# The start of a two-stage kernel: decoding w_in and the first values' maxima placed behind the keys' and queries' maxima, and idle products in place of products on fresh exponentials

## The chip, the cores and the metric

The kernel runs on one core of a Trainium2 chip. The metric is the device time of one execution in microseconds (us). Before the change the median of 3 runs is 954.96 us (954.61 to 955.23).

## What is computed

The reference is attention with random features, followed by a two-layer network with Mish as its activation. Batch 8, 8 heads, 576 positions, head size 64, 128 features; the network takes 4608 rows of 512 and has 2048 hidden units.

```python
def phi(x):
    h = einsum('bhsd,md->bhsm', x, omega) - sum(x * x) / 2
    return exp(h - max(h)) / sqrt(m)
q_p, k_p = phi(q * scale), phi(k * scale)
kv  = einsum('bhsm,bhsd->bhmd', k_p, v);   z = sum(k_p, axis=2)
num = einsum('bhsm,bhmd->bhsd', q_p, kv);  den = einsum('bhsm,bhm->bhs', q_p, z) + 1e-6
x = (num / den), as 4608 x 512
h = x @ w_in
out = (h * tanh(log1p(exp(h)))) @ w_out
```

The two weights arrive as float64, 8 MB each, and are read as integer words.

## The kernel before

**Stages.** Rows are taken in tiles of 128 (q0, q1, ...) and in chunks of 256 (two tiles) for the network. Keys come in pairs of heads: k0 to k3 of the first batch, then k1_0 to k1_3 of the second, and so on. Of a pair of heads, TensorE makes the products with omega (`pk`, line 377), VectorE takes the maximum of each group (`mxk`, line 387), ScalarE makes the exponentials from it (`ek`, line 392), and TensorE multiplies these with the values (`pkv`, line 451); ScalarE copies the sum to SBUF (`kvf`). A tile of queries goes the same way (`pq`, `mxq`, `eq`), and then through `q_first`: transposes of the exponentials (`pt`, line 626), ScalarE's copy (`qp`), the products with kvf (`pn`, line 637), and VectorE's division (`rd`, `x`, lines 641 to 647). x of q0 and q1 is transposed (`px`, `xT`), and with it begins the network's first chunk in f32: `ph`, line 731, takes the decoded blocks of w_in. Its result is copied to the tile `g`. The later chunks use three f16 products each with a weight split in two, for which the scale `s_w` must be known.

**The weights.** A block of w_in (8 of 1024 words per partition, `w_task`) is decoded in four steps: ScalarE's Prelu on the high word (line 184), VectorE's shift of the low word (line 186), VectorE's shift and or (line 190), and VectorE's maximum over the block (`wmax`, line 194). The eight maxima give `am_w` and `s_w`. The tiles are called w_103 to w_110, in the rows of the order with their number, in the trace `w`; the raw words lie in `wo` (the first four) or `raw`.

**The values.** `v_task` takes the maxima of the four value tiles (`vmx`, line 285), then their maximum (`vam`), and from it the scale `s_v` through GpSimd.

**What sets the order.** Every engine works through its instructions strictly in the order in which they are queued. Tasks are Python generators that are stepped in slots: the number they yield says in how many slots they go on. `FIRST` gives the slots of the attention's tasks, `WIS` those of w_in's blocks. Inside these, a scheduler orders the instructions by its own estimates, except that an instruction issued inside `behind(nth)` is put behind the anchors of task nth on the same schedule. An anchor is a pair: the task's last exponential and its last maximum. 3 is the last pair of heads of the first batch, 5 is q1, 31 is the division of q1's x, 101 the second copy of xT. `AV` holds the anchor for `vmx`, `AN` the one of each block for lines 186 and 190, `AM` for line 194, `AP` for line 184; None leaves an instruction free.

**Spare products.** `spin(n, left, right)`, line 96, issues n products that nobody reads. `spin(1, ident, e[:, 0:2])`, line 404, follows the exponentials of the tasks 2 to 5 (k2, k3, q0, q1) and so waits for them. Eight others with the constant tile `idle` stand behind the second pair's products (line 383).

**Buffers that matter.** The exponentials' tile `e` has two buffers; the pool `ps_a` has four PSUM slots, which pk, pq, pkv, pt and pn share.

Of the kernel before, what the change touches and what calls it, by code (L numbers as in the profile page):

```python
# [30 lines left out]
def tile_kernel(  # L31
# [10 lines left out]
    nc = tc.nc  # L42
    P = 128
# [49 lines left out]
    idle = const.tile([P, 512], F16, name="idle")  # L93
    dve.memset(idle, 1.0)

    def spin(n, left, right):
        pi = ps_o.tile([P, 512], F32, tag="o", name=f"spin{nc.next_id()}")
        for _ in range(n):
            nc.tensor.matmul(out=pi[:, 0:right.shape[1]], lhsT=left, rhs=right, start=True, stop=True)
# [3 lines left out]
    ident = const.tile([P, P], F32, name="ident")  # L103
# [156 lines left out]
    for i in range(2):  # L260
        t = const.tile([P, 2, 10, D1], F16, name=f"vb{i}")
# [13 lines left out]
    def v_task(b):  # L275
        vt = []
        for hp in range(HP):
            vt.append(loaded.pop(f"v{b}_{hp}", None) or fetch_v(b, hp))
        if b == 0:
            vstate[0] = (vt, None, None)  # L280
        yield 3 if b else 6
        mx = sb.tile([P, HP], F32, tag="vmx", name=f"vmx{b}", bufs=2)
        for hp in range(HP):
            with behind(AV if b == 0 else None, 1):
                dve.tensor_reduce(
                    out=mx[:, hp:hp + 1], in_=vt[hp][:, :, 0:D], axis=AX.XY, op=ALU.max,
                    apply_absolute_value=True,
                )
            yield 0 if hp % 2 == 0 or b == 0 else 1
        am = sb.tile([P, 1], F32, tag="vam", name=f"vam{b}")  # L290
        with tc.high_priority(PRIO):
            dve.tensor_reduce(out=am, in_=mx, axis=AX.X, op=ALU.max)
            p, s = pow2(am, f"v{b}", TOP)
        vstate[b] = (vt, p, s)
# [42 lines left out]
    def features(load, tiles, name, nth, whole):  # L337

        f = loaded.pop(name, None) or (
            fetch_pair if whole else fetch_tails if name[0] == "k" else fetch
        )(load, name)
        yield gap("load", name)
        if not whole:
            terms = yield from in_parts(f, name, nth)
        n = sum(len(g) for g in tiles)
        by_act = whole
        e = sb.tile([P, n, M], F32, tag="ae", name=f"e{name}", bufs=2)
        mx = sb.tile([P, n], F32, tag="mx", name=f"mx{name}")  # L350
        pps, lo = [], 0
        for g in tiles:
            own, tag = (ps_h, "h") if nth < HP and len(pps) == 2 else (ps_a, "a")
            pp = own.tile([P, 4, M], F32, tag=tag, name=f"p{name}_{lo}")
            pps.append((pp, lo, lo + len(g)))
            lo += len(g)
            if whole:
                continue
            for i, parts in enumerate(g):
                for rows, o in parts:  # L360
                    for j, (left, right) in enumerate(terms):
                        nc.tensor.matmul(  # L362
                            out=pp[rows, i, :], lhsT=left[:, o:o + rows.stop - rows.start],
                            rhs=right, start=j == 0, stop=j == len(terms) - 1,
                        )
        if whole:

            w = f.shape[1]
            order = [(g, i) for i in range(4) for g in (0, -1)] + [(1, 0)] * (len(tiles) - 2)
            mm = None  # L370
            for g, i in order:
                for rows, o in tiles[g][i]:
                    a = slice(o // w * D, (o // w + 1) * D)
                    with ExitStack() as st:
                        if mm is not None:
                            st.enter_context(tc.issue_after(mm.ins))
                        mm = nc.tensor.matmul(
                            out=pps[g][0][rows, i, :], lhsT=f[a, o % w:o % w + rows.stop - rows.start],
                            rhs=om_f[a], start=True, stop=True,
                        )  # L380
            if nth == 1:
                with tc.issue_after(mm.ins):
                    spin(8, idle[:, 0:P], idle)
        yield 1
        for pp, lo, hi in pps:
            m = hi - lo
            sub = dve.tensor_reduce(  # L387
                out=mx[:, lo:hi], in_=pp[:, :m, :], axis=AX.X, op=ALU.max, negate=by_act
            )
            if by_act:  # L390
                for i in range(m):
                    last = act.activation(
                        e[:, lo + i, :], pp[:, i, :], AF.Exp, bias=mx[:, lo + i:lo + i + 1]
                    )
            else:
                sub = dve.tensor_tensor(  # L396
                    out=e[:, lo:hi, :], in0=pp[:, :m, :],
                    in1=mx[:, lo:hi].unsqueeze(2).broadcast_to([P, m, M]), op=ALU.subtract,
                )
        yield gap("exp", name)  # L400
        if not by_act:
            last = act.activation(e, e, AF.Exp, bias=lnt)  # L402
        elif 1 < nth < 6:
            spin(1, ident, e[:, 0:2, :].rearrange("p n m -> p (n m)"))
        anchors[nth] = (last.ins, sub.ins)
        return e

# [211 lines left out]
    def q_first(nth, t, e, off):  # L619

        qp = sb.tile([P, H, P], F32, tag="ap", name=f"qp{t}", bufs=2)
        for g in range(2):
            hs = slice(4 * g, 4 * g + 4)
            pt = ps_a.tile([P, 4, P], F32, tag="a", name=f"pt{t}_{g}")
            for i in range(4):
                nc.tensor.transpose(out=pt[:, i, :], in_=e[:, 4 * g + i, :], identity=ident)
            cast(act, qp[:, hs, :], pt)
        yield 1
        x = sb.tile([P, H, D], F32, tag="x", name=f"x{t}", bufs=2)
        rd = sb.tile([P, H, 1], F32, tag="rd", name=f"rd{t}")  # L630
        for g in range(2):
            hs = slice(4 * g, 4 * g + 4)
            pn = ps_a.tile([P, 4, D1], F32, tag="a", name=f"pn{t}_{g}", padded_shape=[P, 4, P])
            for i in range(4):
                for b, lo, hi in spans(t * P, P):
                    must(HP, "kvf", b)
                    nc.tensor.matmul(
                        out=pn[lo:hi, i, :], lhsT=qp[:, 4 * g + i, lo:hi], rhs=kvf[b][:, 4 * g + i, :],
                        start=True, stop=True,
                    )  # L640
            dve.tensor_scalar(
                out=rd[:, hs], in0=pn[:, :, D:D1], scalar1=EPS, scalar2=1.0 if t * P < CH else TOP / TX,
                op0=ALU.add, op1=ALU.mult,
            )
            dve.reciprocal(out=rd[:, hs], in_=rd[:, hs])
            if t * P < CH:
                xt = dve.tensor_tensor(
                    out=x[:, hs, :], in0=pn[:, :, 0:D], in1=rd[:, hs].broadcast_to([P, 4, D]),
                    op=ALU.mult,
                )  # L650
                continue
            for b, lo, hi in spans(t * P, P):
                xt = dve.scalar_tensor_tensor(
                    out=x[lo:hi, hs, :], in0=pn[lo:hi, :, 0:D], scalar=vstate[b][2][lo:hi],
                    in1=rd[lo:hi, hs].broadcast_to([hi - lo, 4, D]), op0=ALU.mult, op1=ALU.mult,
                )
        anchors[30 + t] = (xt.ins,)
        if t * P >= CH:
            yield from x_parts(nth, t, x)
            return  # L660
        yield 1
        px = ps_a.tile([P, KT, P], F32, tag="a", name=f"px{t}")
        for i in range(KT):
            nc.tensor.transpose(out=px[:, i, :], in_=x[:, 2 * i:2 * i + 2, :], identity=ident)
        last = act.activation(xT0()[:, :, off:off + P], px, AF.Copy)
        anchors[100 + t] = (last.ins,)
        did("x", 0)
        if t == 1:
            for hs in (slice(0, 4), slice(4, 8)):
                spin(1, ident, x[:, hs, :].rearrange("p h d -> p (h d)"))  # L670
# [265 lines left out]
    w_dma = nc.sync  # L936

    FIRST = (0, 1, 2, 3, 4, 4, 9, 9, 19, 21, 24, 27, 32, 36, 43, 58, 59, 68)
    WIS = (3, 4, 5, 6, 7, 8, 9, 10)
    WOS = (28, 27, 26, 25, 24, 23, 22, 21)  # L940
    WI0, FF0, V0, V1 = 0, 17, 0, 16
    W_LOAD, W_GAP, PRIO = 1, 1, 400

    AO = (None,) * 8
    AV = 3
    AN = (None,) * 5 + (31,) * 3
    AM = (None,) * 3 + (31,) * 5
    AP = (None,) * 7 + (101,)

    W_LO = ('dddddddd', 'dddddddd')  # L950
    W_HI = ('aaaaaaaa', 'aaaaaaaa')
# [90 lines left out]
    for what in PREL.split():  # L1042
        i = int(what[1:] or 0)
# [100 lines left out]
```

## Time and profile before

| | |
|---|---|
| median of 3 runs | 954.96 us |
| profiled execution | 955.38 us, its span 953.6 us, mean granted clock 0.989 |
| PE (TensorE) busy | 929.1 us, 97% of the span |
| DVE (VectorE) busy | 625.7 us, 66% |
| ACT (ScalarE) busy | 636.8 us, 67% |
| POOL (GpSimd) busy | 220.6 us, 23% |
| DMA | 100.25 MB, mean 105 GB/s |
| first 20 us | PE 18.53, DVE 7.67, ACT 10.65 us busy |

The chain that ended last, followed back from the last instruction, names `po`, the second layer's products of line 900, with 12% of the span, and PE with 22% in all. Over the whole span TensorE is nearly always busy; the stretch that the change touches is the first 60 us of 954. All times in the text are counted from the start of the span. Instructions of one kind that follow each other stand in one row of the timeline, with their count behind an x; an f32 product is recorded as two instructions. "PEclk" is the clock that TensorE was granted, as a share of full speed.

### The profile page before, as it was taken

The numbers are of one execution on the slowest core, as the hardware profiler recorded it, in microseconds if no ns is written. First come the engines' busy times: TensorE is split into PE (matmuls) and PEld (weight loads), VectorE is DVE, ScalarE is ACT, GpSimd is POOL, SyncE is SP. The second block draws the span as 40 slices with busy tenths as digits, with TensorE's granted clock in tenths as the row PEclk, the third lists the DMA queues.
The fourth block names the chain that finished last, engine by engine and source line by source line (L and its number), as shares of the span: only waits on it lengthen the run. The fifth ranks groups of instructions, "written<-read, shape, count | busy, mean of one in ns | idle before, by whom it ended". The sixth has DMA issues, their size and how long they took to land. (4 is left out here: it accounts for less than half of the span.)

```text
span 953.6 us, 20400 instructions
## 1 busy us (share of the span) xinstructions
PE 929.1 (97%) x8558; PEld 667.8 (70%) x8558; DVE 625.7 (66%) x1080; ACT 636.8 (67%) x821; POOL 220.6 (23%) x141
## 2 busy tenths in 40 slices
PE   9799989999999999999999999999999999999998
PEld 6688765676777777777777777777756777776663
DVE  4799887686665766656564664789889656643330
ACT  5668975678878777787677775778686866432231
POOL 0000042344333222332232323313232231100000
PEclk9799999999999999999999999999999999999999
DMA  9766333432532355224332353324542155644410
GB/s 307 255 221 213 96 82 82 92 82 61 131 79 63 84 104 103 60 62 93 72 68 73 73 114 70 83 78 104 123 113 67 34 115 106 169 129 130 128 63 25
DMA packets 148443, 100.25 MB, mean 105 GB/s; under 512 B 112320, under 2 KB 124736, under 8 KB 148352
## 3 DMA queue, kind: packets, MB, share of 16 engines
q1 hardware_dynamic: 148032, 98.36, 40.7%
q8 instruction: 67, 1.10, 0.5%
q10 hardware_dynamic: 320, 0.59, 0.2%
q14 instruction: 24, 0.20, 0.1%
HBM read 58.95 MB, written 13.63 MB: 76 GB/s over the span
## 5 line engine op out<-in xcount | busy, mean ns | idle before, releaser
L900 PE MATMUL po<-wo,g 128*128 128x512 f16 x1632 | 375.2, 380 | 0.0
L731 PE MATMUL ph<-xT,w 128*128 128x256 f16 (+1 forms) x2816 | 343.9, 278 | 2.7 <-ACT h L876 2.7
L731 PEld LDWEIGHTS <-w 128*128 128x128 f16 x2688 | 261.8, 98 | 51.4 <-issue 4.1
L900 PEld LDWEIGHTS <-g 128*128 128x128 f16 x1632 | 155.2, 98 | 163.9 <-issue 2.2
L83 DVE SCALAR_TENSOR_TENSOR g<-h,us,g 128x1024 f16<-128x1024 f32 (+3 forms) x92 | 117.5, 1287 | 35.8 <-ACT g L72 35.2
L876 ACT ACTIVATE h<-ph,us 128x512 f32<-128x512 f32 (+3 forms) x152 | 83.2, 572 | 75.0 <-PE ph L731 74.1
L81 POOL TENSOR_TENSOR sq<-fq,sq 64x1024 f16<-64x1024 f32 x31 | 69.3, 2238 | 159.1 <-issue 86.8
L81 POOL TENSOR_TENSOR sk<-fk,sk 64x1152 f16<-64x1152 f32 x24 | 60.5, 2519 | 124.1 <-ACT sk L72 99.6
L81 POOL TENSOR_TENSOR xs<-x,xs 128x512 f16<-128x512 f32 (+1 forms) x35 | 43.4, 1241 | 145.1 <-issue 66.7
L72 ACT ACTIVATE g<-h,us 128x1024 f16<-128x1024 f32 (+3 forms) x80 | 72.6, 932 | 1.2
L876 ACT ACT_TABLE_LOAD x56 | 71.8, 1283 | 1.0
L402 ACT ACT_TABLE_LOAD x53 | 68.0, 1283 | 4.2 <-DVE ek L396 3.3
L387 DVE TENSOR_REDUCE mxq<-pq 128x4 f32<-128x512 f32 x72 | 46.8, 681 | 26.6 <-PE pq L362 25.7
L81 DVE TENSOR_TENSOR qn<-eq,qn 128x1024 f16<-128x1024 f32 x31 | 39.5, 1275 | 37.2 <-ACT qn L72 37.2
L834 PEld LDWEIGHTS <-w 128*128 128x128 f16 x1008 | 58.4, 98 | 5.9
L387 DVE TENSOR_REDUCE mxk<-pk 128x4 f32<-128x512 f32 (+1 forms) x96 | 49.5, 548 | 17.7 <-PE pk L362 8.3
L876 ACT ACTIVATE h<-h,us 128x1024 f32<-128x1024 f32 (+2 forms) x16 | 14.7, 933 | 62.0 <-DVE h L843 62.0
L72 ACT ACTIVATE o<-po,us 128x512 f32<-128x512 f32 (+1 forms) x38 | 25.8, 679 | 40.5 <-PE po L900 40.5
L81 DVE TENSOR_TENSOR kp<-ek,kp 128x1152 f16<-128x1152 f32 x24 | 36.8, 1534 | 24.0 <-ACT kp L72 24.0
L402 ACT ACTIVATE eq<-eq,lnt 128x1024 f32<-128x1024 f32 x31 | 35.6, 1148 | 22.1 <-DVE eq L396 21.9
L843 DVE TENSOR_TENSOR h<-p_s,h 128x512 f32<-128x512 f32 x30 | 20.2, 689 | 43.2 <-PE p_s L834 43.2
L81 POOL TENSOR_TENSOR vb<-vf,vb 128x640 f16<-128x640 f32 x24 | 38.7, 1614 | 41.9 <-DVE vb L74 28.1
(143 smaller groups left out, 1140.2 us busy)
## 6 DMA issues: line engine op xcount, KB each, us to landing
w<-ds SPq DMA_DIRECT2D x48, 256.0 KB, 3.4
vf<-in_vL_dram SPq DMA_DIRECT2D x32, 325.0 KB, 3.3
out_dram<-o SPq DMA_DIRECT2D x36, 256.0 KB, 2.3
fq<-in_qT_dram SPq DMA_DIRECT2D x31, 256.0 KB, 3.5
fk<-in_kT_dram SPq DMA_DIRECT2D x24, 256.0 KB, 3.6
raw<-in_w_out_dram SPq DMA_DIRECT2D x5, 1024.0 KB, 7.9
wo<-in_w_in_dram SPq DMA_DIRECT2D x4, 1024.0 KB, 10.7
raw<-in_w_in_dram SPq DMA_DIRECT2D x4, 1024.0 KB, 15.3
```

What stands on the lines that cost most here:

```text
L72: act.activation(out, in_, AF.Copy, scale=scale)
L81: eng.tensor_tensor(out=out, in0=in_, in1=hi, op=ALU.subtract)
L83: eng.scalar_tensor_tensor(out=out, in0=in_, scalar=scale, in1=hi, op0=ALU.mult, op1=ALU.subtract)
L387: sub = dve.tensor_reduce(out=mx[:, lo:hi], in_=pp[:, :m, :], axis=AX.X, op=ALU.max, negate=by_act)
L402: last = act.activation(e, e, AF.Exp, bias=lnt)
L731: nc.tensor.matmul(out=ph[:, i, :], lhsT=wi(a, k, f) if c else wi0(k, f), rhs=xT[c][:, y, k, :] if c else xT0()[:, k, :], start=n == 0, st ...
L834: nc.tensor.matmul(out=ph[:, i, :], lhsT=left(gr, op_l, i, a, k), rhs=x_region(c, r)[:, y, k0 + k, :], start=n == 0, stop=n == len(mm) - 1,)
L843: dve.tensor_tensor(out=out, in0=bank, in1=in0, op=ALU.add)
L876: act.activation(h[:, :, lo:hi], ph[:, :, lo:hi], AF.Mish, scale=us[:, 0:1])
L900: nc.tensor.matmul(out=po[i], lhsT=gT[c, gr][:, a, f % FG, i * P:(i + 1) * P], rhs=wo(y, f), start=f == 0 and (a, y) == parts[0], stop=f = ...
```

## The change

The change edits three places and one group of tables:

- Line 281: the values' task of the first batch goes on one slot later (7 for 6).
- Lines 403 and 404: the product on the fresh exponentials of k2, k3, q0 and q1 is gone.
- In `q_first`, for q0 and q1: 6 and 3 products on the constant tile `idle`, behind the tile's last transpose.
- The tables: w_in's blocks start one or two slots later; `vmx` stands behind q1's maxima; lines 186 and 190 of block 0 stand behind k3's maxima, of block 1 behind q1's, and of the six others behind q1's x; line 194 of block 0 behind k3's maxima, and of all others behind q1's x; the Prelu of blocks 2 to 6 behind q1's last exponential and maximum.

```diff
-        yield 3 if b else 6
+        yield 3 if b else 7
...
             last = act.activation(e, e, AF.Exp, bias=lnt)
-        elif 1 < nth < 6:
-            spin(1, ident, e[:, 0:2, :].rearrange("p n m -> p (n m)"))
         anchors[nth] = (last.ins, sub.ins)
...
-                nc.tensor.transpose(out=pt[:, i, :], in_=e[:, 4 * g + i, :], identity=ident)
+                tr = nc.tensor.transpose(out=pt[:, i, :], in_=e[:, 4 * g + i, :], identity=ident)
             cast(act, qp[:, hs, :], pt)
+        if t < 2:
+            with tc.issue_after(tr.ins):
+                spin(6 - 3 * t, idle[:, 0:P], idle)
...
-    AV = 3
-    AN = (None,) * 5 + (31,) * 3
-    AM = (None,) * 3 + (31,) * 5
-    AP = (None,) * 7 + (101,)
+    AV = 5
+    AN = (3, 5) + (31,) * 6
+    AM = (3,) + (31,) * 7
+    AP = (None,) * 2 + (5,) * 5 + (101,)
```

VectorE's row from the last maximum of k3 to the first of q0, before (mxk_3 is k3's, mxq_330 q0's; w_104 is block 1 of w_in, w_105 block 2):

```order
L387 TENSOR_REDUCE mxk_3_283<-pk_3_5_286 128x4
L285 TENSOR_REDUCE vmx_353<-vf_0_135 128x1
L285 TENSOR_REDUCE vmx_353<-vf_1_137 128x1
L285 TENSOR_REDUCE vmx_353<-vf_2_139 128x1
L285 TENSOR_REDUCE vmx_353<-vf_3_141 128x1
L190 SCALAR_TENSOR_TENSOR w_104<-wo,w_104 128x1024
L292 TENSOR_REDUCE vam_358<-vmx_353 128x1
L186 TENSOR_SCALAR w_105<-wo 128x1024
L134 TENSOR_SCALAR p_v_362<-allm_v_360 128x1
L194 TENSOR_REDUCE wmax_121<-w_104 128x1
L123 TENSOR_SCALAR p_v_362<-p_v_362 128x1
L387 TENSOR_REDUCE mxq_330<-pq_0_331 128x4
```

The same place now, on VectorE, from k3's last maximum on (mxq_320 is q0, mxq_332 q1):

```order
L387 TENSOR_REDUCE mxk_3_278<-pk_3_5_281 128x4
L190 SCALAR_TENSOR_TENSOR w_103<-wo,w_103 128x1024
L194 TENSOR_REDUCE wmax_121<-w_103 128x1
L387 TENSOR_REDUCE mxq_320<-pq_0_321 128x4
L387 TENSOR_REDUCE mxq_320<-pq_4_322 128x4
L387 TENSOR_REDUCE mxq_332<-pq_0_333 128x4
L387 TENSOR_REDUCE mxq_332<-pq_4_334 128x4
L285 TENSOR_REDUCE vmx_416<-vf_0_135 128x1
```

The four maxima of the queries moved ahead of the values' maxima and of blocks 1 and 2. Block 0's lines 190 and 194, which now stand ahead of the queries, stood a few rows further up, between k3's maxima.

TensorE's row behind the products pq of q0 and q1, before (`spin` is a spare product, and what stands behind its arrow is what it reads):

```order
L377 MATMUL pq_4_344<-om_f,fq_146 128x128
L99 MATMUL spin_395<-eq_329,ident 128x256
L451 MATMUL pkv_3_373<-vf_3_141,ek_3_282 128x65 x10
L626 MATMUL pt_0_398<-ident,eq_329 128x128 x4
L99 MATMUL spin_421<-eq_341,ident 128x256
L626 MATMUL pt_1_404<-ident,eq_329 128x128 x4
L626 MATMUL pt_0_424<-ident,eq_341 128x128 x4
L626 MATMUL pt_1_430<-ident,eq_341 128x128 x4
L637 MATMUL pn_0_443<-kvf_162,qp_397 128x65 x4
```

The same place on TensorE now, up to the idle products behind q0's transposes:

```order
L377 MATMUL pq_4_334<-om_f,fq_146 128x128
L449 MATMUL pkv_3_346<-vf_3_141,ek_3_277 128x65 x10
L624 MATMUL pt_0_368<-ident,eq_319 128x128 x4
L624 MATMUL pt_1_374<-ident,eq_319 128x128 x4
L99 LDWEIGHTS idle
L99 MATMUL spin_381<-idle 128x512
L99 LDWEIGHTS idle
L99 MATMUL spin_381<-idle 128x512
```

The product on q0's exponentials ahead of pkv is gone, so is the one on q1's between q0's two groups of transposes, and six idle products follow q0's second group; three more follow q1's.

On VectorE, behind the last part of q1's x, stood before (x_459 is q1's):

```order
L647 TENSOR_TENSOR x_459<-pn_1_469,rd_460 128x256
L194 TENSOR_REDUCE wmax_121<-w_106 128x1
L194 TENSOR_REDUCE wmax_121<-w_107 128x1
L186 TENSOR_SCALAR w_108<-raw_155 128x1024
L186 TENSOR_SCALAR w_109<-raw_157 128x1024
```

And there stands now, on VectorE, behind q1's x:

```order
L648 TENSOR_TENSOR x_452<-pn_1_462,rd_453 128x256
L194 TENSOR_REDUCE wmax_121<-w_104 128x1
L186 TENSOR_SCALAR w_105<-wo 128x1024
L186 TENSOR_SCALAR w_106<-wo 128x1024
L190 SCALAR_TENSOR_TENSOR w_105<-wo,w_105 128x1024
L190 SCALAR_TENSOR_TENSOR w_106<-wo,w_106 128x1024
L194 TENSOR_REDUCE wmax_121<-w_105 128x1
L194 TENSOR_REDUCE wmax_121<-w_106 128x1
L186 TENSOR_SCALAR w_107<-raw_153 128x1024
```

Behind x come now the decoding of blocks 2 and 3 and the shift of block 4, which stood ahead of it. On TensorE, in the first chunk's products ph, 13 of blocks 0 and 1 stand ahead of the products pq of q2, where one stood.

More of the change, by code (lines that the diff above doesn't have):

```diff
@@ L938, in tile_kernel @@
     FIRST = (0, 1, 2, 3, 4, 4, 9, 9, 19, 21, 24, 27, 32, 36, 43, 58, 59, 68)
-    WIS = (3, 4, 5, 6, 7, 8, 9, 10)
+    WIS = (4, 6, 7, 8, 9, 10, 11, 12)
     WOS = (28, 27, 26, 25, 24, 23, 22, 21)
```

## The prediction, made before the run

> **What bounds the kernel now.** I read the busy time by stretch first, then TensorE's waits, then the timeline of 14 to 50 us, and last its later parts. The rows of busy time are cut at the steps of the granted clock, which come every 3.41 us; behind each stretch stand its length, the busy time of PE, PEld, DVE, ACT and POOL with instructions, the granted clock and the DMA share.
>
> ```profile
> 23.81:27.22 3.41, 0.07 (x2) 0.00 (x0) 3.41 (x7) 2.69 (x4) 0.00 (x0) 1.00 1.05 388
> 27.22:30.63 3.41, 0.00 (x0) 0.00 (x0) 3.14 (x8) 0.52 (x3) 0.62 (x1) 0.50 1.05 389
> 30.63:34.05 3.42, 3.26 (x14) 3.08 (x14) 3.42 (x7) 2.69 (x8) 0.00 (x0) 0.50 1.05 385
> 34.05:37.46 3.41, 3.41 (x15) 3.08 (x16) 3.31 (x4) 1.02 (x3) 0.00 (x0) 0.50 1.07 267
> 37.46:40.87 3.41, 3.41 (x16) 2.69 (x14) 0.40 (x1) 2.83 (x9) 0.00 (x0) 0.50 1.03 327
> ...
> 45.53:94.44 48.91, 48.44 (x316) 40.24 (x315) 47.05 (x74) 37.10 (x69) 0.70 (x2) 1.00 0.65 212
> ...
> 94.44:163.80 69.36, 64.39 (x453) 43.38 (x451) 56.68 (x104) 53.03 (x76) 15.68 (x10) 0.98 0.33 85
> ...
> 133.04:136.45 3.41, 0.92 (x9) 0.82 (x9) 2.69 (x5) 3.38 (x5) 1.99 (x2) 1.00 0.38 94
> 136.45:139.86 3.41, 3.41 (x19) 2.42 (x17) 1.08 (x3) 2.31 (x3) 1.34 (x1) 0.50 0.62 175
> ```
>
> TensorE stands still from 23.9 to 30.8 us and then runs at half clock until 40.87. From 45.53 to 94.44 both TensorE (48.44 of 48.91) and VectorE (47.05) are full, so a gain made ahead of that stretch has to pass two full engines. The waits of TensorE name who holds it (total, times, longest):
>
> ```profile
> PE spin L99 <- ACT eq L392: 6.9, 1, 6.9
> ...
> PE ph L731 <- ACT h L876: 2.7, 1, 2.7
> PE pn L533 <- DMA qp<-qn: 1.8, 1, 1.8
> ```
>
> ScalarE's exponentials of q0 are late, and ScalarE itself waits. The timeline says for what (start, length, engine, line, operation; in brackets idle time and releaser):
>
> ```profile
> 18.75 0.69 DVE L387 TENSOR_REDUCE mxk<-pk 128x4 f32<-128x512 f32 x1 [1.36 <-PE pk L377]
> 18.96 2.44 PE L451 MATMUL pkv<-vf,ek 128*128 128x65 f32 x20
> ...
> 21.24 0.65 PE L99 MATMUL spin<-ek,ident 128*128 128x256 f32 x2
> ...
> 21.82 2.06 PE L377 MATMUL pq<-om_f,fq 64*128 64x128 f32 x32
> ...
> 23.02 2.99 DVE L285 TENSOR_REDUCE vmx<-vf 128x1 f32<-128x640 f32 x4
> ...
> 25.92 1.22 DVE L190 SCALAR_TENSOR_TENSOR w<-wo,w 128x1024 int32<-128x1024 int32 x1
> ...
> 27.12 0.68 DVE L186 TENSOR_SCALAR w<-wo 128x1024 int32<-128x1024 int32 x1
> ...
> 28.15 1.21 DVE L194 TENSOR_REDUCE wmax<-w 128x1 f32<-128x1024 f32 x1
> ...
> 29.33 0.68 DVE L387 TENSOR_REDUCE mxq<-pq 128x4 f32<-128x512 f32 x1
> ...
> 30.11 2.17 ACT L392 ACTIVATE eq<-pq,mxq 128x128 f32<-128x128 f32 x8 [3.09 <-DVE s_v L125]
> ...
> 30.79 1.22 PE L99 MATMUL spin<-eq,ident 128*128 128x256 f32 x2 [6.92 <-ACT eq L392]
> ...
> 31.80 4.37 PE L451 MATMUL pkv<-vf,ek 128*128 128x65 f32 x20
> ...
> 40.69 3.77 PE L637 MATMUL pn<-kvf,qp 128*128 128x65 f32 x32
> ...
> 45.11 0.42 DVE L647 TENSOR_TENSOR x<-pn,rd 128x256 f32<-128x256 f32 x1
> ...
> 46.98 0.70 PE L731 MATMUL ph<-xT,w 128*128 128x256 f32 x2
> ```
>
> The products pq of both queries are done at 23.88, but VectorE works through the values' maxima and the decoding of w_in first and takes their maxima only at 29.33. Behind that, pkv takes 4.37 us at half clock where it took 2.44 at full, and the first hidden products ph start at 46.98.
>
> **The change, part by part.** The sum goes against the profiled execution: 955.38 us, of which 953.6 is the span and 1.8 lies around it. The median of the runs is 954.96, so 0.42 comes off at the end. 0.2% is 1.9 us, about what a measurement here can tell from no change.
>
> *Maxima first.* The first maximum of k3 moves up by the dropped product on exponentials ahead of pk: 18.75 - 0.65 = 18.1. The three maxima follow each other (0.6, 0.2, 0.6) to 19.5; one L190 and one wmax stay ahead of the queries. Neighbouring rows overlap by a little under 0.1 us (wmax from 28.15 would end at 29.36, yet q0's maximum starts at 29.33), so a step of 1.22 counts 1.13 and one of 0.68 counts 0.6: to 21.8; the queries' maxima follow. From maximum to exponential is 30.11 - 29.33 = 0.78, so eq starts at 22.65 instead of 30.11: 7.5 us earlier.
>
> *No product on exponentials ahead of pkv.* pkv of k3 still waits for the first four exponentials, since it takes the PSUM slot of pq; four of 2.17 / 8 = 0.27 end at 23.8. TensorE's pause shrinks from 6.92 to about 1 us, pkv runs at 2.44 and ends at 26.3 instead of 36.2.
>
> *Idle products.* Six behind q0's transposes and three behind q1's cost, by these rows from elsewhere in the profile (eight of the same shape; four transposes at full clock):
>
> ```profile
> 9.17 1.90 PE L99 MATMUL spin<-idle 128*128 128x512 f16 x8
> ...
> 57.74 0.60 PE L626 MATMUL pt<-ident,eq 128*128 128x128 f32 x4
> ...
> 71.65 7.17 PE L731 MATMUL ph<-xT,w 128*128 128x256 f32 x32
> ```
>
> 9 x 0.24 = 2.1 us, against 4 x 0.60 of transposes. Most of it lies in the wait for q1's exponentials: its buffer comes free with pkv's end, so they run from 26.4 to 28.6, and the transposes of q1 end near 30.9. Uncovered is the last group of three, 0.7. So pn starts at 31.55 where it was 40.69, 9.1 earlier, x is done 4.84 behind it (45.53 - 40.69) at 36.4 and, with one decoding Prelu of ScalarE now ahead of the last copy of xT, ph starts at 38.2, 8.8 earlier.
>
> *What VectorE owes then.* Behind x now stand five steps of 1.13 and three of 0.6 more than before, 7.45 us. VectorE is thus at the old point of its work at 36.4 + 7.45 = 43.85 instead of 45.53: a lead of 1.7 where TensorE leads by 8.8. The wait for w blocks is short (TensorE multiplies the first blocks while VectorE decodes the next, some 0.5 us lost). Eleven ph instructions of 7.17 / 16 = 0.45 now precede pn of q2, 4.9 us of work, and pn of q2 starts near 57.8 instead of 61.17: a lead of 8.3. It breaks at the first head of the second batch:
>
> ```profile
> 61.17 3.68 PE L637 MATMUL pn<-kvf,qp 128*128 128x65 f32 x32
> ...
> 74.22 1.48 DVE L387 TENSOR_REDUCE mxk<-pk 128x4 f32<-128x512 f32 x3
> ...
> 77.50 2.43 ACT L392 ACTIVATE ek<-pk,mxk 128x128 f32<-128x128 f32 x9
> ...
> 78.76 1.52 PE L377 MATMUL pk<-om_f,fk 64*128 64x128 f32 x18
> ...
> 80.21 2.45 PE L451 MATMUL pkv<-vf,ek 128*128 128x65 f32 x20
> ```
>
> Before, the exponentials end at 79.93 and pkv follows at 80.21, without a pause. After, VectorE reaches these maxima near 71.8 and ScalarE ends near 77.3, only 2.6 earlier, while TensorE has nothing left from 70.1: I get a new pause of 4.7 us, to 74.8. This is the change's own bill. The lead is 2.9 at the next pkv and 1.9 where the f16 products begin (94.44 before, 92.6 after).
>
> *The later waits.* From 94.44 to the start of q7's products (the last row below) the orders of all engines come together again, so what stands there stays to the end.
>
> ```profile
> 135.53 4.44 PE L731 MATMUL ph<-xT,w 128*128 128x256 f16 x24 [2.66 <-ACT h L876]
> ...
> 145.18 0.92 PE L533 MATMUL pn<-kv,qp 128*128 128x65 f16 x24 [1.77 <-DMA qp<-qn]
> ...
> 163.80 1.05 PE L362 MATMUL pq<-om,sq 128*128 128x128 f16 x16
> ```
>
> TensorE has 64.39 us of work there in 69.36, and 1.7 of the work is the second half-clock window (136.45 to 139.86, behind a window with 0.92 busy). At full clock it is 62.7. In the new order the third head's exponentials follow the second's with no Mish between, two of ScalarE's table changes fewer, and eq of q4 comes near 110 instead of 115; I keep 1.2 for the transposing DMA ahead of pn and 0.5 for the rest. 92.6 + 62.7 + 1.7 = 157.0 against 163.8: 6.8 earlier.
>
> *The clock.* The new pause of 4.7 us can cover a clock step. The rows show that a step with 0.07 or 0.92 us busy is followed by half clock, and this pause leaves such a step for most positions of the steps. The price has two ends: one step of 3.41, half of it lost, 1.7 (136.45), or four steps as from 27.22, three of them with work, 5.1. I take 1.7: as at 136.45, long runs of ph stand right behind.
>
> The Trainium skill, page "TensorE: Matmul & The Clock Gate", section "Part 1: The HAM clock gate", says that the clock halves after one idle window of some 3.4 us and returns after one busy one, with windows that run free of the kernel. By that rule the pause would cost an estimated 1.7 us. The first half of the rule agrees with 27.22 and 136.45; the second differs from the rows of 30.63 and 34.05, busy 3.26 and 3.41 us and followed by half clock all the same.
>
> Sum: -6.8 + 1.7 = -5.1, so 950.3 profiled, 949.9 as a median; I say 950.0. What lies outside these terms I cost at nothing: the decoded blocks' scale comes near 61.8 instead of 61.1, hidden by the f32 chunk, which uses no scaled block.
>
> **The rivals.**
>
> *VectorE alone decides (0.20).* With 47.05 of 48.91 busy it passes on only its own 1.7 us, and the later waits stay, since they hang on ScalarE, which waits for VectorE's splits. 955.38 - 1.7 - 0.42 = 953.3. For it: the full row. Against: VectorE idles 12.7 of the 69.36 us from 94.44.
>
> *The whole lead survives (0.12).* If the head's exponentials come as early as TensorE does, 8.8 stays: 954.96 - 8.8 = 946.2. Against it: the chain through ScalarE's Mish and two table loads ahead of 77.50.
>
> *The half clock feeds itself (0.10).* The pause near 70 to 75 halves the clock, and the f32 products of the second batch, of the kind that stayed at half clock from 30.63 on, don't lift it; every head's pause prolongs it. Each step costs 1.7, so from the fifth it is slower than before in the sum (6.8 - 8.5); six, to about 95 us, give 954.96 - 6.8 + 10.2 = 958.4. The page's rule, one busy window and it is over, speaks against so many; the rows of 30.63 to 40.87 speak for it.
>
> *It doesn't do what it says (0.08).* pkv still waits for q0's exponentials through its PSUM slot; if these come no earlier, because w0's decoding or its load holds VectorE ahead of them, only the dropped products count: within a microsecond of 955.
>
> **How the numbers follow.** The forecast has 0.50, with its own range of 948.0 to 952.5 (clock price 0 to 3.4, the pause off by a microsecond). Faster by over 0.2% means under 953.05: the forecast, the second rival and over half of the first, 0.74. Within: the rest of the first, most of the fourth, 0.15. Slower: the third and a little of the fourth, 0.11. The range, 946.5 to 956.0, leaves out the edge of the second rival and most of the third.
>
> **What would show it.** Right: eq near 22.7, pkv at 2.44 us, clock 1.00 from 14 to 60, ph at 38, a pause of TensorE of some 5 us at 70 to 75 released by ek, and q7's products near 158 to 159. Wrong: TensorE paused by w blocks between 40 and 60 (VectorE decides), no pause at 70 (the lead survives), clock 0.50 for over 14 us (slower), or eq still near 30.

## The result, and the profile after

The changed kernel takes 961.88 us (median of 6 runs, 959.89 to 963.64), the kernel before, on the same chip, 955.10 (6 runs, 954.19 to 955.66). The ratio is 1.0072 with a 95% interval of 1.0058 to 1.0086: slower by 0.7%, where 950.0 was forecast. The profiled execution took 961.23 us, its span 959.4 against 953.6 before. One run of e3 below, 1066.19 us at a granted clock of 0.849 where every other run here has 0.981 or more, is left out of its ratio.

The start went as forecast. TensorE's rows in the timeline of the kernel after:

```profile
23.92 2.45 PE L449 MATMUL pkv<-vf,ek 128*128 128x65 f32 x20 [1.12 <-ACT eq L392]
...
30.88 3.68 PE L638 MATMUL pn<-kvf,qp 128*128 128x65 f32 x32
...
37.19 1.13 PE L732 MATMUL ph<-xT,w 128*128 128x256 f32 x4 [0.79 <-ACT xT L666]
...
72.30 1.52 PE L377 MATMUL pk<-om_f,fk 64*128 64x128 f32 x18 [2.19 <-ACT ek L392]
74.99 4.53 PE L449 MATMUL pkv<-vf,ek 128*128 128x65 f32 x20 [1.17 <-ACT ek L392]
...
86.09 2.45 PE L449 MATMUL pkv<-vf,ek 128*128 128x65 f32 x20
```

The first 6.9 us of waiting are down to 1.12, pkv runs at full clock, and ph starts at 37.19 instead of 46.98: 9.8 us earlier. At 72 to 75 the new pause stands, 2.19 + 1.17 us, released by ek. At the second batch's next pkv (86.09, before 87.83) 1.7 us of the lead are left. Up to here nothing is slower than before.

The loss comes later. TensorE's rows of the kernel after, around the tiles q5, q6 and q7 (before: pn of q5 at 145.18, pn of q6 at 163.04, pq of q7 at 163.80):

```profile
136.63 1.50 PE L531 MATMUL pn<-kv,qp 128*128 128x65 f16 x24 [2.88 <-DMA qp<-qn]
137.94 1.85 PE L362 MATMUL pq<-om,sq 128*128 128x128 f16 x16
139.63 13.95 PE L918 MATMUL po<-wo,g 128*128 128x512 f32 x32
157.39 1.50 PE L531 MATMUL pn<-kv,qp 128*128 128x65 f16 x24 [3.81 <-DMA qp<-qn]
158.70 5.21 PE L918 MATMUL po<-wo,g 128*128 128x512 f32 x6
163.74 3.60 PE L918 MATMUL po<-w,g 128*128 128x512 f32 x8
167.18 1.06 PE L362 MATMUL pq<-om,sq 128*128 128x128 f16 x16
```

pn of q5 now starts 8.6 us earlier than before, so the early lead is there. But pn of q6 then waits 3.81 us for its transposing DMA, with 14 records of po (6 and 8, 8.8 us of work) queued behind it that need nothing from it. They run after the wait, and q7's products start at 167.18, 3.4 us later than before. The waits of TensorE between 100 and 200 us say the same in a row:

```profile
PE pn L531 <- DMA qp<-qn: 6.7, 2, 3.8
```

Before, the two were 1.8 and 0.55. In the changed kernel one step of half clock follows the first of them, two the second. Busy time by stretch of the kernel after, at the steps of the clock (columns as in the prediction):

```profile
74.78:78.19 3.41, 3.20 (x15) 3.20 (x16) 3.41 (x5) 3.26 (x4) 0.00 (x0) 0.50 0.61 203
78.19:81.61 3.42, 3.05 (x11) 2.48 (x11) 3.42 (x6) 2.05 (x7) 0.00 (x0) 0.50 0.30 65
81.61:85.02 3.41, 3.41 (x13) 2.38 (x13) 3.41 (x4) 2.56 (x7) 0.00 (x0) 0.50 0.09 33
...
136.20:139.61 3.41, 2.98 (x40) 2.99 (x41) 2.43 (x11) 1.55 (x2) 0.00 (x0) 0.50 0.02 5
...
156.68:160.09 3.41, 2.70 (x26) 2.13 (x27) 1.89 (x6) 0.00 (x0) 0.00 (x0) 0.50 0.63 196
160.09:163.51 3.42, 3.42 (x5) 1.35 (x4) 1.37 (x4) 1.01 (x1) 0.00 (x0) 0.50 0.00 0
```

The first three rows lie behind the new pause at 72 to 75 us. What stands differently is TensorE's row behind the pq of q6. Equal rows are drawn together here, with their count ahead. Before:

```
12 L533 MATMUL pn_1_1376<-kv_674,qp_1318 128x65        (q5)
 8 L362 MATMUL pq_0_1409<-om,sq_1320 128x128           (q6)
 8 L362 MATMUL pq_4_1418<-om,sq_1320 128x128
...
 1 L917 MATMUL po_0_1390<-wo,g_0_634 128x512 x2
 1 L917 MATMUL po_1_1391<-wo,g_0_634 128x512 x2
 1 L917 MATMUL po_0_1390<-w_110,g_0_634 128x512 x2
 1 L917 MATMUL po_1_1391<-w_110,g_0_634 128x512 x2
12 L533 MATMUL pn_0_1460<-kv_674,qp_1450 128x65        (q6)
```

After:

```
 1 L918 MATMUL po_0_1391<-wo,g_0_635 128x512
12 L531 MATMUL pn_0_1461<-kv_675,qp_1451 128x65        (q6)
12 L531 MATMUL pn_1_1474<-kv_675,qp_1451 128x65
 1 L918 MATMUL po_0_1391<-wo,g_0_635 128x512
 1 L918 MATMUL po_1_1392<-wo,g_0_635 128x512 x2
 1 L918 MATMUL po_0_1391<-w_110,g_0_635 128x512 x2
 1 L918 MATMUL po_1_1392<-w_110,g_0_635 128x512 x2
 8 L362 MATMUL pq_0_1534<-om,sq_1520 128x128           (q7)
```

The change doesn't touch this place, 120 us behind its last edit. The scheduler orders by its own estimates, and with the changed start it places pn of q6 ahead of seven po instructions (14 records) behind which it stood before. Which estimate tips it isn't shown.

### The profile page after: what moved, and what is told of

The parts are those of the page before. It is cut to its first block, busy times and chain, and to the rows that moved or that the text cites. A ratio compares the mean times of both kernels' runs of the same rounds, so it can differ in the third digit from the quotient of the medians.

```text
span 959.4 us, 20405 instructions
## 1 busy us (share of the span) xinstructions
PE 931.9 (97%) x8559; PEld 669.5 (70%) x8559; DVE 629.3 (66%) x1080; ACT 633.8 (66%) x819; POOL 225.8 (24%) x141
## 5 line engine op out<-in xcount | busy, mean ns | idle before, releaser
L81 POOL TENSOR_TENSOR xs<-x,xs 128x512 f16<-128x512 f32 (+1 forms) x35 | 45.4, 1297 | 154.6 <-issue 67.5
```

Source lines behind the costliest of these rows:

```text
L81: eng.tensor_tensor(out=out, in0=in_, in1=hi, op=ALU.subtract)
```

## The experiments

Each kernel was timed in five rounds beside the kernel before. Times are medians with the range and the number of runs; "pn of q6", "q7" and "span" are of the profiled execution.

| kernel | median us (range, runs) | ratio to before (95%) | pn of q6 | pq of q7 | span |
|---|---|---|---|---|---|
| before | 955.10 (954.19 to 955.66, 6) | | 163.04 | 163.80 | 953.6 |
| after | 961.88 (959.89 to 963.64, 6) | 1.0072 (1.0058 to 1.0086) | 157.39 | 167.18 | 959.4 |
| e1_spins_only | 960.42 (958.23 to 962.97, 6) | 1.0059 (1.0042 to 1.0075) | 158.59 | 166.27 | 956.4 |
| e2_order_only | 956.46 (954.06 to 959.38, 12) | 1.0013 (1.0002 to 1.0025) | 158.37 | 166.84 | 954.5 |
| e3_warm70 | 959.50 (954.56 to 963.55 and one of 1066.19, 12) | 1.0037 (1.0019 to 1.0056) | 158.06 | 166.36 | 957.7 |
| e4_late6 | 955.54 (951.51 to 958.19, 12) | 0.9998 (0.9982 to 1.0013) | 164.35 | 165.09 | 955.0 |
| e5_before_early6 | 962.59 (960.68 to 967.73, 6) | 1.0086 (1.0065 to 1.0108) | 163.76 | 172.60 | 960.8 |
| e6_order_late6 | 955.07 (953.50 to 958.95, 12) | 1.0000 (0.9987 to 1.0012) | 160.27 | 161.01 | 953.5 |
| e7_spins_late6 | 954.00 (952.70 to 958.03, 12) | 0.9996 (0.9984 to 1.0009) | 162.04 | 162.78 | 952.6 |
| e8_warm70_late6 | 954.22 (948.03 to 957.45, 12) | 0.9985 (0.9968 to 1.0003) | 158.00 | 158.74 | 954.5 |
| e9_after_late56 | 954.38 (951.90 to 957.18, 12) | 0.9996 (0.9982 to 1.0010) | 157.10 | 157.84 | 954.0 |
| e10_warm_late56 | 953.22 (949.91 to 957.37, 12) | 0.9986 (0.9971 to 1.0002) | 155.12 | 155.87 | 954.0 |
| e11_full | 959.30 (956.37 to 960.95, 6) | 1.0044 (1.0027 to 1.0060) | 157.04 | 157.79 | 957.8 |
| e12_before_warm | 956.14 (953.52 to 959.45, 12) | 1.0011 (0.9998 to 1.0025) | 160.20 | 160.95 | 953.5 |
| e13_vmx_late | 950.80 (950.43 to 952.19, 6) | 0.9950 (0.9929 to 0.9970) | 154.52 | 155.27 | 948.9 |
| e14_warm_vmx_late | 950.95 (947.82 to 958.69, 12) | 0.9955 (0.9934 to 0.9976) | 155.26 | 156.01 | 948.5 |
| e15_before_vmx_late | 954.87 (952.27 to 956.67, 12) | 0.9993 (0.9979 to 1.0007) | 163.49 | 164.23 | 954.1 |

### The two halves of the change

e1 is the kernel before with only the spare products changed; e2 is the change with the old spare products. The edit of e1 against before:

```diff
-        elif 1 < nth < 6:
-            spin(1, ident, e[:, 0:2, :].rearrange("p n m -> p (n m)"))
...
+        if t < 2:
+            with tc.issue_after(tr.ins):
+                spin(6 - 3 * t, idle[:, 0:P], idle)
```

> The order tables of before with the changed spare products (none on fresh exponentials, 6 and 3 idle ones behind the transposes). Theory A (what counts is VectorE's order, and the time is lost behind it): the queries' maxima stay at 29 us, TensorE pauses at 24 to 30 as before, and the time stays within 1.5 us of before (954 to 956.5). Rival (the dropped products kept the clock up, and their loss is the cost): slower than before by 3 us or more.

> The changed order tables with the spare products of before. Theory A: ph starts near 37 to 38 us, the pauses at 70 to 75 and ahead of pn of q5 and q6 come as in the changed kernel, 959 to 963 us. Rival (the spare products are to blame): 953 us or less.

e1 is slower by 0.6%, e2 by 0.1%, barely. That the two add up to the 0.7% of the whole looks like a split, but the traces don't read that way. e1 has no lead (ph at 49.30, later than the 46.98 of before), yet pn of q6 stands at 158.59 with po behind it and q7 at 166.27. e2 has the whole lead (ph at 36.21) and q7 at 166.84. In both, as in the whole change, pn of q5 has 18 records of the first chunk's po ahead of it instead of 28, and pn of q6 stands ahead of the last po. So the order of TensorE's row flips with either half, with a lead or without one, and what they have in common is that flip. The flip alone doesn't set its price, though: e2 has it too, with a wait of 3.60 us, and is only 0.1% slower than before. It starts q7 3.0 us late and is 0.9 behind at the end of the span.

### The pause at 70 to 75 us

e3 is the changed kernel with idle products in the pause: nine behind the first pk of k1_1, five ahead of the pkv of k1_0.

```diff
+                if name == "k1_1" and (g, i) == (-1, 0):
+                    with tc.issue_after(mm.ins):
+                        mm = spin(9, idle[:, 0:P], idle)
...
+            if name == "k1_1":
+                with tc.issue_after(mm.ins):
+                    spin(5, idle[:, 0:P], idle)
```

> The changed kernel with 14 more idle products: 9 behind the first product pk of k1_1, 5 between pk of k1_1 and pkv of k1_0, where TensorE pauses for 2.2 and 1.2 us. Theory A (the half clock from 75 to 85 us takes 5 us of TensorE's lead, and what it takes stays lost): clock 1.00 from 14 to 130 us, pkv of k1_1 near 82 instead of 86, the total 3 to 5 us under the changed kernel (957 to 959). Rival B (VectorE and ScalarE set the pace behind 90 us, so time won there comes back as a longer wait): clock 1.00 too, but the total within 1.5 us of the changed kernel, with longer waits of TensorE from 95 to 165.

pkv runs at 2.45 us again instead of 4.53, and the half clock of that stretch shrinks from three steps to one (two others come in its start, at 24 to 32). The ratio falls from 1.0072 to 1.0037, with intervals that stay apart (1.0058 to 1.0086, 1.0019 to 1.0056). But q7 starts at 166.36, only 0.8 earlier than in the changed kernel, since pn of q6 still waits at its new place, for 3.6 us. The runs of e3 spread with the clock that they were granted: the three at 0.996 took 954.56 to 955.25, level with before, and the five at 0.985 to 0.992 took 959.50 to 963.55, all with pn of q6 in its new place. So much of e3's loss goes with half clock, wherever it falls. It isn't the whole of the slowdown, as e4 shows next at an equal clock.

### The place of q6's products

In the changed kernel, e4 makes q6's task wait more slots ahead of its pn, which puts pn of q6 behind all po of the first chunk, as before the change. e5 does the opposite to the kernel before: it queues the last seven po instructions behind pn of q6, as they stand after the change, holds the third chunk's first ph behind these po (not in the cut below), and changes nothing in the start.

```diff
 # e4, against after
-        yield 2
+        yield {6: 11}.get(t, 2)
...
 # e5, against before
+                    with behind(66 if blk == 0 or blk == 1 and i + f > 2 else None):
+                        mm = nc.tensor.matmul(
```

> The changed kernel with pn of q6 queued 9 slots later, so that it stands behind all products po of the first chunk, as it did before. Theory A (the wait of 3.8 us ahead of it and the two steps of half clock behind it, 3.4, come from its place in TensorE's row): both go, q7's products start near 160 instead of 167, the total 954 to 956. Rival B: the wait is set by a chain of VectorE and DMA that something else needs next; the total falls by less than 2 us.

> The kernel before with one move on TensorE: pn of q6 stands ahead of the last 14 recorded products po of the first chunk (7 instructions), where it stands in the changed kernel; everything ahead of 160 us stays. Theory C (this place costs the time, whatever the start does): TensorE reaches pn of q6 6 us before its transposed operand has landed, waits 6 to 7 us, and the clock halves behind it: 961 to 964 us. Rival D (the place costs only together with a start that runs ahead): 957 us or less.

e4 takes the loss away: 955.54 against 961.88, level with before (0.9982 to 1.0013). TensorE's rows of e4:

```profile
144.53 16.55 PE L918 MATMUL po<-wo,g 128*128 128x512 f32 x38
160.91 3.60 PE L918 MATMUL po<-w,g 128*128 128x512 f32 x8
164.35 0.91 PE L531 MATMUL pn<-kv,qp 128*128 128x65 f16 x24
165.09 1.06 PE L362 MATMUL pq<-om,sq 128*128 128x128 f16 x16
```

pn of q6 follows po without a wait, at full clock (0.91 instead of 1.50). And e5 brings the loss into the kernel before: 962.59 against 955.00. TensorE's rows of e5:

```profile
147.56 9.66 PE L920 MATMUL po<-wo,g 128*128 128x512 f32 x22
163.76 1.50 PE L533 MATMUL pn<-kv,qp 128*128 128x65 f16 x24 [6.54 <-DMA qp<-qn]
165.07 4.25 PE L920 MATMUL po<-wo,g 128*128 128x512 f32 x6
169.16 3.60 PE L920 MATMUL po<-w,g 128*128 128x512 f32 x8
172.60 1.06 PE L362 MATMUL pq<-om,sq 128*128 128x128 f16 x16
```

The wait is 6.54 us and q7 comes at 172.60 instead of 163.80. The two experiments agree in size: -6.3 us by putting pn back, +7.6 by moving it forward. A higher clock doesn't explain it: at a granted clock of 0.985 two runs of the changed kernel took 962.98 and 963.64 us, four of e4 956.43 to 958.19. The place of these 24 products, which the diff doesn't mention, is the cause of the slowdown, by the wait and by the half clock behind it.

The same mend was then made on the two halves (e6 is e2 with it, e7 is e1) and on e3 (e8).

> The changed order tables, the spare products of before, and pn of q6 behind all products po of the first chunk. Theory C: the 6 us that the place of pn took come back, from 956.5 to 950 to 952, so faster than before by 3 to 5 us. Rival E (the lead of the start is lost on the way in any case, to VectorE and ScalarE or to half clock): 954 to 956.

> The order tables of before, the changed spare products, and pn of q6 behind all products po of the first chunk. Theory C (without the tables there is no lead, and without the wrong place no loss): 954 to 956 us. Rival (the changed spare products themselves cost at the start): 958 us or more.

> The changed kernel, the 14 idle products at 70 to 75 us, and pn of q6 behind all products po. Theory A with C (half clock from 75 to 85 takes part of the lead, and the place of pn the rest): under the changed kernel with the late pn alone by 2 to 4 us, 951.5 to 953.5. Rival B (time won at 75 to 85 is waited for later): within 1 us of it, 954.5 to 956.5.

All three are level with before, each interval holding 1.0. So with the mend neither half costs time. The mend takes 6.4 us off e1 and 5.3 off e3, but only 1.4 off e2, where q7 starts 5.8 us earlier and the span still ends only 1.0 earlier. So the price of the place isn't the same in every kernel; why it is so small in e2 wasn't traced. None is faster than before either, although e8 starts q7's products at 158.74, 5.1 us earlier than before. The end of the span hardly moves: from q7's start to the end e8 takes 795.8 us where before takes 789.8. With the first loss mended, the lead is given back a second time, behind q7. In e8 it goes in pieces: 3.0 us are left at the pq that starts at 218.74 before (215.70 in e8), 0.6 at the one of 683.27 (682.71).

### Where the lead goes behind q7

e9 puts pn of q5 back as well (24 records of po ahead of it, 28 before); e10 is e9 with the idle products of e3.

```diff
 # against after
-        yield 2
+        yield {5: 7, 6: 11}.get(t, 2)
```

> The changed kernel with pn of q5 and pn of q6 queued later, so that 12 and 32 instructions po of the first chunk stand ahead of them (8 and 25 in the changed kernel). Theory A (TensorE's own waits and half clock are the loss): the wait of 2.9 us ahead of pn of q5 and the half step behind it, 1.7, go too; 951 to 953 us. Rival B (what is saved ahead of 165 us is waited for behind it): 954.5 to 956.5, as with pn of q6 alone.

> As the run before it, and with the 14 idle products at 70 to 75 us. Theory A: 1.5 to 3 us under it. Rival B: within 1 us of it.

q7 starts at 157.84 and 155.87, 6.0 and 7.9 us earlier than before, and both kernels end level with before again. TensorE's and then VectorE's rows of e10 behind q7's start:

```profile
155.87 1.06 PE L363 MATMUL pq<-om,sq 128*128 128x128 f16 x16
156.76 2.78 PE L739 MATMUL ph<-xT,w 128*128 128x256 f16 x24
165.32 1.01 PE L363 MATMUL pq<-om,sq 128*128 128x128 f16 x8 [5.77 <-DVE rd L549]
166.88 1.03 PE L363 MATMUL pq<-om,sq 128*128 128x128 f16 x8 [0.56 <-DVE x L554]
167.71 2.77 PE L908 MATMUL po<-wo,g 128*128 128x512 f16 x6
```

```profile
159.64 1.66 DVE L286 TENSOR_REDUCE vmx<-vf 128x1 f32<-128x640 f32 x2 [2.11 <-DMA vf<-in_vL_dram]
161.22 3.14 DVE L83 SCALAR_TENSOR_TENSOR wo<-w,s_w,wo 128x1024 f16<-128x1024 f32 x1
164.28 0.15 DVE L549 TENSOR_SCALAR rd<-pn 128x4 f32<-128x4 f32 x1
```

The next products on queries wait 5.77 us for the PSUM slots that rd and x of q6 set free. pn is done near 156, but ahead of rd in VectorE's row stand two maxima of the fourth batch's values (`vmx`), which wait 2.11 us for their load; the splitting step behind them (`wo`, line 83) takes 3.14 us, and rd comes at 164.28. Half clock follows the wait, and by the pq that starts at 218.74 before (219.87 in e10) the lead is gone. Where the load went, the timeline of SyncE's queue says, in e10:

```profile
148.55 3.03 SPq L524 DMA_TRANSPOSE qp<-qn  x1
...
155.57 1.02 SPq L273 DMA_DIRECT2D vf<-in_vL_dram  x2
```

In the kernel before, the same load and the first of its maxima:

```profile
136.01 2.13 SPq L272 DMA_DIRECT2D vf<-in_vL_dram  x2
...
138.87 0.82 DVE L285 TENSOR_REDUCE vmx<-vf 128x1 f32<-128x640 f32 x1 [2.33 <-DMA vf<-in_vL_dram]
```

Before, the load stood ahead of q5's transposing DMA in SyncE's queue and was issued at 136.01; the wait for it lay 25 us ahead of rd of q6. Now it stands behind q6's transposing DMA, one of xT and three loads of keys, and is issued 19.6 us later. This is the second place that the scheduler turned over, and it has a like form: a DMA that needs results of the engines (qn) stands ahead of a load that doesn't.

e11 tries whether the half clock in the start is what eats the lead: it is e10 with four more idle products at the start, so that the first 80 us run at full clock. e12 does the like in the kernel before, with 26 idle products in its pause of 6.9 us.

```diff
 # e12, against before (e11 has 4 for 26, against e10)
-            if nth == 1:
+            if nth in (1, 5):
                 with tc.issue_after(mm.ins):
-                    spin(8, idle[:, 0:P], idle)
+                    spin(8 if nth == 1 else 26, idle[:, 0:P], idle)
```

> As the run before it, and with 4 idle products between pq of q1 and pkv of k3, where TensorE pauses for 1.1 us at 23 us and some executions show half clock from 25 to 32 or 35. Theory A: clock 1.00 through 20 to 130, 948 to 951 us. Rival B: 953.5 to 956.

> The kernel before with 26 idle products in its pause of 24 to 31 us, all else in its old place. The clock stays up, so pkv of k3 takes 2.4 us instead of 4.4, and ph starts near 43.5 instead of 47, with VectorE's order as it was. Theory A (a lead of TensorE at ph reaches the end): 951 to 953 us. Rival B (VectorE and ScalarE, full from 45 to 130, take it back): 954 to 956.

With a granted clock of 0.995 (e11) and 0.996 (e12) they have the highest of all the profiled executions (before 0.989), and neither kernel is faster than before: e12 956.14 with its first ph 2.6 us earlier than before, e11 959.30. But e12's lead isn't lost in the start, nor near q7. Two of TensorE's rows far behind, before and then in e12:

```profile
683.27 1.06 PE L362 MATMUL pq<-om,sq 128*128 128x128 f16 x16
...
743.97 1.17 PE L362 MATMUL pk<-om,sk 128*128 128x128 f16 x18
```

```profile
679.59 1.06 PE L362 MATMUL pq<-om,sq 128*128 128x128 f16 x16
...
743.87 1.17 PE L362 MATMUL pk<-om,sk 128*128 128x128 f16 x18
```

The lead is 2.9 us at q7's start, 3.7 at 680 us and gone at 744. Between these rows TensorE waits 7.6 us in e12 (for VectorE and for a transposing DMA) and 4.2 before. So what a clock won in the start is worth isn't settled by e12. Why e11 is 6 us slower than e10 stays open; its pn of q6 waits 2.85 us and its next pq 4.75, but at the pq of 218.74 it is only 1.2 us behind e10 (221.07, 219.87), and 3.8 at the end of the span.

e13 is e9 with the two waiting maxima put behind x of q6, and e14 is e10 with the same edit. e15 is the control: both mends (pn of q5 and q6, and the maxima) in the kernel before, with its start unchanged.

```diff
-            with behind(AV if b == 0 else None, 1):
+            with behind(AV if b == 0 else 36 if (b, hp) in ((3, 1), (3, 2)) else None, 1 if b == 0 else 0):
...
-            yield 0 if hp % 2 == 0 or b == 0 else 1
+            yield 7 if (b, hp) == (3, 0) else 0 if hp % 2 == 0 or b == 0 else 1
```

> The changed kernel with pn of q5 and q6 late, and the two maxima vmx of the fourth batch's values, which wait for their transfer, placed on VectorE behind x of q6 instead of ahead of it. If VectorE's row ahead of that division gives the lead back: TensorE's pause at 161 to 165 us (3.1 us, then half clock) goes, and the time falls by 3 to 5 us to 950 to 952. If the later part is held by something else: the time stays at 953.5 to 955.5, with a pause elsewhere before 250 us.

> As the run before it, with the 14 idle products at 70 to 75 us. If VectorE's row there gives the lead back: the pause of 5.8 us shrinks to 2 or less and the time is 948 to 951, 1 to 2 us under the run before it. If not: within 1 us of 953.

> The kernel before with the same late places of pn of q5 and q6 and of the two maxima of the fourth batch's values. If the gain of the mended changed kernel is the lead of its start: 954 to 956 us, as before. If the mending brings it by itself: 950 to 952.

TensorE's, then VectorE's rows of e14, to be held against those of e10:

```profile
156.01 1.06 PE L363 MATMUL pq<-om,sq 128*128 128x128 f16 x16
156.90 2.78 PE L739 MATMUL ph<-xT,w 128*128 128x256 f16 x24
160.78 0.61 PE L363 MATMUL pq<-om,sq 128*128 128x128 f16 x8 [1.10 <-DVE rd L549]
162.35 0.62 PE L363 MATMUL pq<-om,sq 128*128 128x128 f16 x8 [0.96 <-DVE x L554]
162.81 2.75 PE L908 MATMUL po<-wo,g 128*128 128x512 f16 x12
```

```profile
158.53 1.28 DVE L83 SCALAR_TENSOR_TENSOR wo<-w,s_w,wo 128x1024 f16<-128x1024 f32 x1 [1.28 <-ACT wo L72]
159.74 0.15 DVE L549 TENSOR_SCALAR rd<-pn 128x4 f32<-128x4 f32 x1
```

q7 starts at the same time as in e10 (156.01, 155.87), the wait for rd falls from 5.77 to 1.10, the po behind comes at 162.81 instead of 167.71, and the span ends at 948.5 instead of 954.0. The medians say the same, less sharply. From e9 to e13 it is 954.38 to 950.80, with intervals apart (0.9982 to 1.0010, 0.9929 to 0.9970). From e10 to e14 it is 953.22 to 950.95, with intervals that overlap, and the two traces exaggerate: e10's profiled execution (955.84) lies 2.6 us above its median. The wait for the load is also only a part of the 4.5 us by which rd comes later in e10 than in e14: of its 2.11 us e14 has 1.28 all the same, waiting for ScalarE. The maxima themselves take 1.66, and the splitting step 3.14 instead of 1.28, with GpSimd at work beside it (160.92 to 163.28).

The control gains nothing (0.9979 to 1.0007): where the load comes early, the two maxima are in nobody's way. So the 0.5% of e13 comes from the changed start, once two places behind it let it through. It isn't the lead of the first 40 us carried along: where the long run of ph begins (91.10 before, 90.07 in e13) 1.0 us of it is left. Behind that, before has waits of 2.66, 1.77 and 0.55 us and a step of half clock, e13 no wait over 0.3 until q7, which it starts 8.5 us earlier; 4.7 of these reach the end of the span. A kernel in which the load itself is put back in SyncE's queue was not tried. e13 is faster than both kernels of this case.

## Why the prediction was wrong, point by point

- **Maxima first, no product ahead of pkv, idle products:** right. eq was forecast at 22.65, came at 22.72; pkv at 2.44, was 2.45; pn at 31.55, came at 30.88; ph at 38.2, came at 37.19.
- **What VectorE owes then:** right in mechanism and place, a pause at 70 to 75 released by ek, and pkv at 74.99 where 74.8 was forecast. The pause of 4.7 us came as two waits of 2.19 and 1.17 with pk between them. The lead at the next pkv was put at 2.9 and is 1.7.
- **The clock:** a mis-sized term. Three steps of half clock, 74.78 to 85.02, at 1.7 each are 5.1, the other end of the bounds, where 1.7 was taken. The trace had rows of both kinds, and the choice went by the wrong one: behind the pause stands pkv with its 65 columns, as at 31.80 before, not a long run of ph. The Trainium skill's rule ("TensorE: Matmul & The Clock Gate", "Part 1: The HAM clock gate") that one busy window brings the clock back would have given one step: the step from 74.78, with 3.20 of 3.41 us busy, is followed by two more at half clock. The last of the three is the first that is busy throughout (3.41), and full clock follows it, so this row contradicts the rule only if 3.20 counts as busy; the row of 34.05 before, 3.41 busy and followed by half clock, contradicts it outright. The other half of the rule speaks of an idle window, and the step ahead of 136.45 was 0.92 us busy, so that row is only near it.
- **The later waits:** this is the step that failed. It read "From 94.44 to the start of q7's products (the last row below) the orders of all engines come together again, so what stands there stays to the end." Neither half holds. The orders don't come together: pn of q6 stands ahead of seven po instructions, its DMA wait grows from 0.55 to 3.81 us with half clock behind it, and q7 comes 3.4 us later instead of 6.8 earlier. e4 and e5 show that this costs 6 to 8 us (in e2, by e6, 1.4). The text had allowed 1.2 for the DMA ahead of pn, from a wait whose place in the row it took as given. The prediction doesn't lay the rows between the two places side by side for the two kernels, though the order of the changed kernel, drawn above, shows the move.
- **"Stays to the end":** e6 to e10 mend the order, start q7 between 155.87 and 162.78, and all end level with before. With pn of q5 and q6 back, q7's start is at 157.84 (e9), close to the 157.0 of the sum; but the values' load now stood behind q6's transposing DMA in SyncE's queue, VectorE's maxima waited for it ahead of rd, and the lead was given back (e9 against e13). The prediction names no queue of loads in that stretch.
- **The rest of the loss:** from q7's start to the end the changed kernel takes 792.2 us against 789.8 before. Of these 2.4 us, 1.9 are lost by the pq that starts at 218.74 before and at 223.98 after: ahead of it two pkv wait 1.15 and 0.41 us for VectorE, where before has no such wait.
- **The rivals:** "the half clock feeds itself" had the right sign and a time not far off (958.4) by a cause that isn't the one: it stops after three steps, and at an equal clock of 0.985 e4 is some 6 us faster than the changed kernel. "VectorE alone decides" (953.3) is near what the mended kernels take (953.2 to 955.5), in part by luck. Its first half fits: at 91 us only 0.4 to 1.0 us of the lead are left (after, e13). Its second half, that the later waits stay, doesn't: without them e13 starts q7 8.5 us earlier, and what the other mended kernels lose, they lose behind q7.
- With the order of the later stages put right, the change is worth about what was forecast, 950.8 in e13 against 950.0. That the numbers meet is partly luck: the sum has 6.8 us at q7's start, less 1.7 for the clock, all of it kept, and e13 has 8.5 there, of which 4.7 are kept.

## What to carry to other kernels

Where a scheduler places instructions by its own estimates, an edit at the start is also an edit of every later stage: lay the rows of each engine side by side to the end of the pipeline, not only where the diff is, and look, on the engines and in the queue of loads, for what waits for a DMA and has moved ahead of work that doesn't need it. A ratio near 1.0 after a large local gain is a reason to look for the place that gives it back, and a control (the same mends without the gain) tells whose gain it is.

## What the runs showed of the hardware

**Half clock without a long pause.** In e4's start the waits of TensorE are hardly longer than in the changed kernel (1.23 us against 1.12), and yet it ran at half clock from 25 to 35 us. TensorE's rows of e4, to be compared with 23.92 of the kernel after:

```profile
21.88 1.16 PE L377 MATMUL pq<-om_f,fq 64*128 64x128 f32 x14 [0.30 <-ACT kvf L72]
24.26 3.79 PE L449 MATMUL pkv<-vf,ek 128*128 128x65 f32 x20 [1.23 <-ACT eq L392]
```

The step ahead of the half clock (21.69 to 25.10) has 2.00 of 3.41 us busy, far from idle, with products of 64 rows or 65 columns. e3, e8 and e9 show the same at 24 to 33 us, while the kernel after, e10, e13 and e14 don't. How long TensorE is busy in a step doesn't decide alone: in e10 a step with 2.57 us busy, mostly pkv of 65 columns, is followed by half clock (75.44 to 78.85), in the kernel after one with 2.16, all ph of 256 columns, by full clock (67.95 to 71.37). Narrow products seem to count as less work; no run here isolates it.

**The clock and the spread of one kernel's runs.** The program is the same, the clock isn't: e10's five runs at a granted clock of 0.994 or more took 949.91 to 951.49 us, its seven at 0.991 or less 953.07 to 957.37; e14's ends are 947.82 at 0.996 and 958.69 at 0.986. A wait can bring half clock and half clock can bring a wait, so this doesn't say which comes first. It does say that a single profiled execution is one draw out of such a spread, and that two kernels are best compared at equal clocks.

**VectorE beside GpSimd.** VectorE's, then GpSimd's rows of the kernel after, on the way to pn of q6:

```profile
147.07 2.24 DVE L83 SCALAR_TENSOR_TENSOR wo<-wo,s_w 128x1024 f16<-128x1024 f32 x1 [0.77 <-ACT wo L72]
149.23 3.15 DVE L81 TENSOR_TENSOR qn<-eq,qn 128x1024 f16<-128x1024 f32 x1
```

```profile
146.10 5.20 POOL L81 TENSOR_TENSOR sq<-fq,sq 64x1024 f16<-64x1024 f32 x2
151.38 4.61 POOL L81 TENSOR_TENSOR vb<-vf,vb 128x640 f16<-128x640 f32 x2
```

The split of qn takes 3.15 us instead of the 1.22 that the same step took at 157.45 before, with GpSimd at rest. The Trainium skill, "SBUF — State Buffer", "SBUF: two separate sides", says that the two engines' shared ports are an exclusive lock, where the later one waits for the whole instruction of the earlier. The row agrees: GpSimd's second sq ends at 151.30, and 1.22 more is 152.52, against the 152.38 at which qn ends. By this the wait of pn of q6 holds an estimated 1.9 us (3.15 less 1.22) that come from qn now standing beside GpSimd's work; no run takes GpSimd's work away to show it.
